# A one-core scan-and-gate kernel: the first loads, the first gate block and one square root are put in another order

## The chip, the cores and the metric

The kernel runs on one core of one Trainium2 chip. The metric is the device time of one execution in microseconds (us); lower is better. A line such as L826 is line 826 of the kernel file. TensorE is written PE (its weight loads PEld), VectorE DVE, ScalarE ACT, GpSimd POOL and SyncE SP. SP and ACT issue the loads that matter here; such an issue is written SPq or ACTq in the profile.

## The reference

The input is 2048 tokens of 448 numbers. After a layer norm, two branches read the same rows: a gated feed-forward block, and a diagonal complex recurrence over all tokens.

```
xn = layernorm(x)                                # x: 2048 x 448
g  = sigmoid(xn @ w_gate);  u = xn @ w_up        # w_gate, w_up: 448 x 1792
B  = silu((g * u) @ w_down)                      # w_down: 1792 x 448
h[t] = Lam_bar * h[t-1] + (xn @ B_bar.T)[t]      # complex, 448 states
A  = 2 * real(h @ C.T) + xn * Dskip
out = x + A * B
```

## The kernel before, in words

The tokens are cut into 4 chunks of 512, and each chunk into 4 tiles of 128 rows. PE works through chunk 0's gate products, then its up products, then the products of the recurrence, then the later chunks, nearly without a gap. The 1792 columns of `w_gate` are 14 blocks of 128, held as two halves: columns 0 to 895 lie on partitions 0 to 63 and columns 896 to 1791 on partitions 64 to 127. The 448 rows of the weights are seven row blocks `s` of 64 rows. A product `m` is a pair of streams, L808 with L809 (or L826 with L827), one on each half of the partitions, over the seven `s`.

The change lies in the head, the time until PE has its first full-width product (L808 on 512 columns, which starts at 10.71 us in the profile). What happens there:

- Loads of `x`, one for each 128-row tile 0 to 3, two issued by SP (0, 2) and two by ACT (1, 3).
- Gate block 0 (products `m` = 0 and 1, 256 columns of each half, 448 KB in all) comes in four pieces made by `load_w0`. Of half 0, part A holds `s` = 1, 3, 5 and part B `s` = 0, 2, 4, 6; of half 1 it is the other way round. The A pieces (96 and 128 KB) are what the "b" products of tile 0 read; the "a" products read the B pieces too. One A piece goes through ACT, the rest through SP.
- Gate blocks 1 (224 KB a half) and 2 (336 KB a half) follow on SP's queue, then more of `x`, then the up weights.
- Tiles 0, 2 and 3 get their mean and variance on DVE (`bn`, L451; `aggr`, L457). Tile 1 gets them on ACT: `act_mean` (L489) and `act_var` (L493), each a pass over 448 columns.
- The standard deviation of a tile is a small ACT instruction: `root` (L485), or `act_root` (L497) for tile 1. DVE then takes the reciprocal (`recip`, L482) and writes the normalised tile (`norm`, L531).
- PE transposes the normalised tile 0 (L569, L571). ACT copies slots 4 to 6 out of PSUM first, and slots 0 to 3 second (both L579, "copy b" and "copy a" in this text). With copy b, PE can do tile 0's "b" products (L826, L827 with `s` = 1, 3, 5), with copy a the "a" products.
- Between the two groups of products PE transposes tile 1 (L589, L590), behind them tiles 2 and 3, each copied out by ACT (L593); DVE shifts rows for tiles 1 to 3 (L600). Then come the products of tiles 1, 2 and 3.
- A small copy on ACT (L642, `pv`) feeds a chain on POOL (L653 to L659) whose result two ACT passes (`scale`, L669) need; behind these ACT loads its silu table (L665) and clears the first gate products from PSUM (L842).

While `pl.seq` is true (from `stats(0)` to `scale(3)`), the order of the instructions on DVE and ACT is the order of the Python calls; PE's order is always that, and so are SP's and ACT's loads. All the rest on DVE, ACT and POOL is put in order by a planner, `Plan.solve`, from costs and due times. For loads, the planner takes the landing time that `land=` names; it sets an order, not a time on the chip. A load issued by SP or ACT uses one of eight semaphores in turn, so the ninth waits until the first has landed.

Of the kernel before, what the change touches and what calls it, by code (L numbers as in the profile page):

```python
# [14 lines left out]
ACT = mybir.ActivationFunctionType  # L15
# [5 lines left out]
P = 128  # L21
H = 64
# [51 lines left out]
class Plan:  # L74
# [10 lines left out]
    def add(self, eng, cost, fn, r=(), w=(), dma=0, lat=None, chain=False, name="", rate=230e3):  # L85
        o = Op()
        o.idx, o.eng, o.cost, o.fn, o.dma, o.name = len(self.ops), eng, cost, fn, dma, name
        o.lat = LAT.get(eng, 0.0) if lat is None else lat
        o.pre, o.suc, o.rate = {}, [], rate
        o.slot, o.land = None, 0.0  # L90
        if dma and eng != "POOL":
            o.slot, self.n_dma = self.n_dma, self.n_dma + 1
        o.start = o.end = None
        for k in r:
            if k in self.w:
                self._edge(self.w[k], o, True)
        for k in w:
            for q in self.r.get(k, ()):
                self._edge(q, o, False)
            if k in self.w:  # L100
                self._edge(self.w[k], o, True)
        for k in w:
            self.w[k] = o
            self.r[k] = []
        for k in r:
            if k not in w:
                self.r.setdefault(k, []).append(o)
        if chain or eng == "PE" or (eng in ("DVE", "ACT") and self.seq):
# [138 lines left out]
def kernel(  # L247
# [18 lines left out]
    V, A, G, T, Q = nc.vector, nc.scalar, nc.gpsimd, nc.tensor, nc.sync  # L266
# [5 lines left out]
    def sbt(name, shape, dt=BF16):  # L272
        return sb.tile([P] + list(shape), dt, name=name)
# [10 lines left out]
    wgt = {"g": sbt("wG", [7, 896]), "u": sbt("wU", [7, 896])}  # L284
    wsrc = {"g": B_w_gate, "u": B_w_up}
# [5 lines left out]
    xnT = [flat(t[:], 7, L) for t in xnT_raw]  # L291
# [55 lines left out]
    gu = [pp.tile([P, 2, 512], FP32, name=f"gu{i}") for i in range(3)]  # L347
# [3 lines left out]
    add = pl.add  # L351
# [14 lines left out]
    def load_w(eng, k, half, b, r=(), rate=105e3, land=0.0):  # L366
        m0, m1 = BLK[k][b]
        ps = slice(half * H, half * H + H)
        c0 = half * 896
        load(eng, [("w", k, half, m) for m in range(m0, m1)], H * 7 * (m1 - m0) * P * 2,  # L370
             wgt[k][ps, :, m0 * P:m1 * P],
             wsrc[k][:, c0 + m0 * P:c0 + m1 * P].rearrange("(s p) f -> p s f", p=H), cost=0.65, r=r, rate=rate, land=land)

    def load_w0(eng, half, part, r=(), land=0.0):
        ps = slice(half * H, half * H + H)
        s0, c0 = (1 - half if part == "A" else half), half * 896
        n = 4 - s0
        load(eng, [("w", "g", half, m, part) for m in range(2)], H * n * 2 * P * 2, wgt["g"][ps, s0:7:2, 0:2 * P],
             wsrc["g"][:, c0:c0 + 2 * P].rearrange("(s p) f -> p s f", p=H)[:, s0:7:2, :], cost=0.5, r=r, rate=400e3, land=land)

    def wkeys(k, m, part=None):
        if k == "u" or m > 1:
            return [("w", k, 0, m), ("w", k, 1, m)]
        if part == "b":
            return [("w", k, 0, m, "A"), ("w", k, 1, m, "A")]
        return [("w", k, h, m, q) for h in range(2) for q in "AB"]

    def load_wd(h):
        fs = slice(h * 7, h * 7 + 7)
# [11 lines left out]
    def load_p(eng, k, r=()):  # L401
        load(eng, ("vrow", k), D * 2, vrow[k:k + 1, :], (A_log_dt, A_Lambda_im, A_Lambda_re)[k].unsqueeze(0), cost=0.75 if eng == "POOL" else 0.45, r=r)
    load_x(0, 1, "SP")
    load_x(1, 1, "ACT")
    load_x(2, 1, "SP", rate=180e3)
    load_x(3, 1, "ACT", rate=180e3)
    load_p("SP", 2)
    add("ACT", 0.05, lambda: A.preload_act_table_set("sqrt_and_others"), w=["sqrttab"], lat=1.3, chain=True)
    load_w0("SP", 0, "A", land=5.7)
    load_w0("ACT", 1, "A", land=5.9)  # L410
    load_w0("SP", 0, "B", land=6.9)
    load_w0("SP", 1, "B", r=[("x", 1)], land=6.9)
    load_p("POOL", 0)
    load_p("POOL", 1)
    add("POOL", 0.15, lambda: G.memset(ident[:], 0.0), w=["ident"], chain=True)
    add("POOL", 0.4, lambda: G.affine_select(out=ident[:], in_=ident[:], compare_op=ALU.not_equal, fill=1.0, base=0,
                                             pattern=[[-1, P]], channel_multiplier=1), r=["ident"], w=["ident"], chain=True)
    add("POOL", 0.1, lambda: G.memset(wgt["g"][0:1, 0, 256:258], 0.0), w=[("w", "g", 0, m) for m in (2, 3)], chain=True)
    load_w("SP", "g", 0, 1, rate=400e3, land=8.8)
    load_w("SP", "g", 1, 1, rate=400e3, land=9.8)  # L420
    load_w("SP", "g", 0, 2, rate=400e3, land=11.2)
    load_w("SP", "g", 1, 2, rate=400e3, land=12.6)
    load_x(4, 2, land=14.0)
    add("POOL", 0.1, lambda: G.memset(halfc[:], 0.5), w=["consts"])
    add("POOL", 0.1, lambda: G.memset(negc[:], -1.0), r=["consts"], w=["consts"])
    add("POOL", 0.1, lambda: G.memset(expc[:], math.e), w=["expc"])
# [5 lines left out]
        w=[("xnw", t) for t in (1, 2, 3)])  # L432
# [26 lines left out]
    def stats(t):  # L459
        bn(t)  # L460
        aggr(t)
# [22 lines left out]
    def root(t):  # L484
        add("ACT", 0.2, lambda: A.activation(sdb[:, t, :], mvf[:, t, 1:2], ACT.Sqrt, bias=epsc[:]),  # L485
            r=[("mv", t), "sqrttab", "epsc"], w=[("sd", t)], lat=0.16)

    def act_mean(t):
        add("ACT", 0.62, lambda: A.activation(junk[:], x_all[:, t, :], ACT.Identity, scale=-1.0 / D, accum_out=nmf[:, t, :]),  # L489
            r=[("x", t), "sqrttab"], w=[("nf", t), "junk"])  # L490
# [324 lines left out]
    def last_tile(c, k, steps, j, hs="ba"):  # L815
        x, w_ = xnT[c % 3], wgt[k]
        ts = slice(j * P, j * P + P)
        for h in hs:
            ss = {"a": (0, 2, 4, 6), "b": (1, 3, 5), "c": (0, 2, 4), 1: (6,)}[h]
            for m, a in steps:  # L820
                ms = slice(m * P, m * P + P)

                def f(ms=ms, a=a, ss=ss):
                    for s in ss:
                        go, end = (s == 1, s == 6) if hs[0] == "b" or hs == "a" else (s == 0, s == 5)
                        T.matmul(gu[a][:, 0, ts], lhsT=w_[0:H, s, ms], rhs=x[0:H, SL[s], ts], start=go, stop=end)  # L826
                        T.matmul(gu[a][:, 1, ts], lhsT=w_[H:P, (s + 1) % 7, ms], rhs=x[H:P, SL[s], ts], start=go, stop=end)  # L827
                add("PE", len(ss) * 0.0562, f, r=[("xnT", c % 3, j, "a" if h == "c" else h)] + wkeys(k, m, "b" if h == "b" else "a"), w=[("gu", a)],
                    name=f"{k}{c}.{m}")

    sg_n = [0]
# [227 lines left out]
    def yout(c, j, first=False):  # L1059
        t = c * TPC + j  # L1060
        g, o, q = gt_of[c, j], next_o(), t % NXD
        a = next_acc()
        key, ok, od = ("acc", a), ("o", o, 0), o_t[o][:]
        y = y_mm(c, j, acc[a], key, 0, D, False, first)
        add("DVE", dve1(D), lambda: V.tensor_tensor(out=od, in0=y, in1=xd[q][:], op=ALU.add), r=[key, ("xd", q)], w=[ok])
        add("DVE", dve2(D), lambda: V.tensor_tensor(out=od, in0=od, in1=g_t[g][:], op=ALU.mult), r=[ok, ("gt", g)], w=[ok])
        add("DVE", dve2(D), lambda: V.tensor_tensor(out=od, in0=od, in1=x_all[:, t, :], op=ALU.add), r=[ok, ("x", t)], w=[ok])
        rows = (0, H, P) if c == 2 and j == 3 else (0, P)
        for r0, r1 in zip(rows, rows[1:]):
            store(t, od, 0, D, r0, r1, [ok])  # L1070

# [31 lines left out]
    u2 = slots0[2]  # L1103
    gate([("gu", u2)], [("gu", u2, 0), ("gu", u2, 1)])
    stats(0)
    act_mean(1)
    bn(2)
    root(0)
    act_var(1)
    recip(0, 1)  # L1110
    aggr(2)
    norm(0)
    act_root(1)
    root(2)
    stats(3)
    recip(1, 1)
    norm(1)
# [1 line left out]
    def split(t, keys, banks, eng, between=None):  # L1119
        pe_transpose(t, [(4, 7, keys[0], banks[0], eng[0]), (0, 4, keys[1], banks[1], eng[1])], between)  # L1120
# [5 lines left out]
    def between_copies():  # L1126
        copies.append(columns(acc[1][:, 400:412], ("acc", 1)))
        last_tile(0, "g", steps01, 0, "b")
        root(3)
    split(0, ak, ab, ("ACT", "ACT"), between_copies)  # L1130
    copies[0]()
    add("NONE", 0.0, lambda: None, r=["pv0", ("xn", 1)], w=["pv"], lat=0.0)
    first_slots(1, uk[0], ub[0], "ACT")
# [94 lines left out]
    a = next_acc()  # L1228
# [37 lines left out]
```

## Time and profile before

| | |
|---|---|
| three runs | 182.92, 183.3, 183.31 us; median 183.3 |
| profiled execution: span, first to last instruction | 181.5 us |
| median of the runs above that span | 1.8 us |
| PE busy | 177.1 us, 98% of the span |
| DVE, ACT, POOL busy | 92%, 54%, 21% |
| granted TensorE clock | 1.00 throughout |
| PE idle in the last stage, 170 to 181.5 us | 3.07 us of 11.5 |

The profile gives no device time of the profiled execution besides its span, so sums are made against that span and carried over to the median of the runs by their difference.

How to read what follows: in the timeline an entry gives start, duration, engine, line, what it writes and reads, and in brackets how long the engine sat idle before it and what ended that. In the table of stretches each engine has its busy time in the stretch.

### The profile page before, as it was taken

The page shows a single profiled execution, that of the slowest core. Times are in us where ns is not written, and L with a number is a line of the kernel's source. Part 1 is how long each engine was busy: PE and PEld are TensorE (multiplying, and loading weights), DVE is VectorE, ACT ScalarE, POOL GpSimd, SP SyncE. Part 2 cuts the span into 40 slices and gives each one's busy share as a digit, 9 for nine tenths or more (in the row PEclk, how much of TensorE's full clock was granted, in tenths as well). Part 3 has the DMA queues.
Part 4 walks back from the last instruction along what each step waited for, and adds up shares of the span by engine and source line. Part 5 has one row for each costly group of instructions (what it writes and reads, how often), then busy time and mean ns, then how long its engine had stood idle before and what let it go on. Part 6 is the DMA issues. An engine that isn't in the chain of part 4 may idle for free.

```text
span 181.5 us, 3611 instructions
## 1 busy us (share of the span) xinstructions
PE 177.1 (98%) x1404; PEld 88.2 (49%) x1411; DVE 166.4 (92%) x294; ACT 98.2 (54%) x162; POOL 37.6 (21%) x94
## 2 busy tenths in 40 slices
PE   8999999999999999999999999999999999999993
PEld 2664445664544444445554444444555444455552
DVE  3778799999989999999999999999999999999772
ACT  5799998857699985364155543348110533411100
POOL 6472468100018797000004100000000000000000
PEclk9999999999999999999999999999999999999999
DMA  5999999999000290000004900002000000002121
GB/s 133 227 224 229 160 165 207 252 242 257 23 0 0 52 148 6 0 4 0 0 2 88 143 0 0 4 0 69 7 4 0 25 27 28 1 0 76 47 65 47
DMA packets 30853, 13.43 MB, mean 74 GB/s; under 512 B 19442, under 2 KB 30835, under 8 KB 30835
## 3 DMA queue, kind: packets, MB, share of 16 engines
q1 hardware_dynamic: 30210, 12.83, 34.9%
q10 hardware_dynamic: 560, 0.36, 0.7%
q8 instruction: 11, 0.18, 0.5%
q14 instruction: 8, 0.06, 0.1%
q0 software_dynamic: 64, 0.00, 0.0%
HBM read 6.77 MB, written 1.84 MB: 47 GB/s over the span
## 4 chain that ended last, share of the span: by engine, by line
PE 94%; DMA 2%; SPq 1%; DVE 1%; issue 0%; DVEq 0%
PE gu L808 43%; PE gu L1024 15%; PE acc L1043 11%; PE acc L1024 9%; PE gu L896 8%; DMA wG<-in_B_w_gate_dram 2%; PE acc L899 2%; PE gu L882 2%; SPq L357 1%; PE gu L826 1%; PE acc L808 1%; PE gu L809 1%; DVE o_t L1085 0%; PE gu L827 0%; DVE o_t L1079 0%
## 5 line engine op out<-in xcount | busy, mean ns | idle before, releaser
L808 PE MATMUL gu<-xnT,wU 64*128 64x512 bf16 x196 | 45.8, 376 | 0.0
L809 PE MATMUL gu<-xnT,wU 64*128 64x512 bf16 x196 | 45.8, 376 | 0.0
L808 PE MATMUL gu<-xnT,wG 64*128 64x512 bf16 (+1 forms) x189 | 41.3, 360 | 0.0
L809 PE MATMUL gu<-xnT,wG 64*128 64x512 bf16 (+1 forms) x189 | 41.3, 360 | 0.0
L842 ACT ACTIVATE sig<-gu 128x1024 f32<-128x1024 f32 x21 | 21.3, 1019 | 24.4 <-PE gu L809 19.8
L1024 PEld LDWEIGHTS <-hF 128*128 128x128 bf16 x224 | 21.9, 98 | 20.6
L808 PEld LDWEIGHTS <-wU 64*128 64x128 bf16 x196 | 18.4, 94 | 22.9
L808 PEld LDWEIGHTS <-wG 64*128 64x128 bf16 x196 | 18.4, 94 | 19.9
L1024 PE MATMUL gu<-wd,hF 128*128 128x448 bf16 x140 | 28.0, 352 | 0.0
L845 DVE SCALAR_TENSOR_TENSOR hF<-sig,gu 128x1024 bf16<-128x1024 f32 x21 | 25.4, 1210 | 0.7 <-ACT sig L842 0.4
L1043 PE MATMUL acc<-cT,hT 128*128 128x448 bf16 (+2 forms) x119 | 22.9, 337 | 0.0
L963 DVE TENSOR_TENSOR_SCAN wv<-c_r,st,z 128x512 bf16<-128x512 f32 x18 | 22.8, 1273 | 0.0
L1030 ACT ACTIVATE g_t<-gu 128x448 bf16<-128x448 f32 x10 | 5.4, 540 | 27.7 <-PE gu L1024 16.8
L809 PEld LDWEIGHTS <-wU 64*128 64x128 bf16 x196 | 18.4, 94 | 0.0
L809 PEld LDWEIGHTS <-wG 64*128 64x128 bf16 x196 | 18.4, 94 | 0.0
L1024 PE MATMUL acc<-wd,hF 128*128 128x448 bf16 x84 | 16.9, 352 | 0.0
L1043 PEld LDWEIGHTS <-hT 128*128 128x128 bf16 x126 | 11.7, 98 | 9.9 <-issue 0.4
L896 PE MATMUL gu<-xnT,bT 128*128 128x512 bf16 x65 | 15.3, 379 | 0.4
L910 ACT CAST bus<-gu 128x1024 bf16<-128x1024 f32 x12 | 12.0, 1011 | 5.9 <-PE gu L882 5.3
L541 POOL COPY xn<-xn 128x448 bf16<-128x448 bf16 x12 | 7.5, 627 | 27.2 <-ACT xn L535 27.0
L916 ACT CAST bus<-acc 64x256 bf16<-64x256 f32 (+1 forms) x24 | 8.7, 368 | 4.8 <-PE acc L899 4.5
L535 ACT ACTIVATE xn<-x_all,nmr,rsd 128x448 bf16<-128x448 bf16 x12 | 8.8, 758 | 3.7 <-DVE xd L546 2.2
(162 smaller groups left out, 263.1 us busy)
## 6 DMA issues: line engine op xcount, KB each, us to landing
wd<-in_B_w_down_dram SPq DMA_DIRECT2D x2, 784.0 KB, 6.6
out_dram<-o_t SPq DMA_DIRECT2D x14, 112.0 KB, 1.7
wU<-in_B_w_up_dram SPq DMA_DIRECT2D x4, 224.0 KB, 8.4
x_all<-in_A_x_dram SPq DMA_DIRECT2D x2, 448.0 KB, 5.0
wG<-in_B_w_gate_dram SPq DMA_DIRECT2D x2, 336.0 KB, 5.4
wU<-in_B_w_up_dram SPq DMA_DIRECT2D x2, 336.0 KB, 8.5
wG<-in_B_w_gate_dram SPq DMA_DIRECT2D x2, 224.0 KB, 4.1
x_all<-in_A_x_dram SPq DMA_DIRECT2D x2, 224.0 KB, 7.7
```

Source lines behind the costliest of these rows:

```text
L535: add("ACT", 0.65, lambda: A.activation(o[:, 0:448], x_all[:, t, :], ACT.Identity, bias=nmr[:, t, :], scale=rsd[:, t, :]), r=[("x", t), (" ...
L541: add("POOL", 0.25 if n == H else 0.6, lambda: G.tensor_copy(out=o[:, D:D + n], in_=o[:, 0:n]), r=[("xn", b)], w=[("xnw", b)])
L808: T.matmul(bank[0][:, ts], lhsT=w_[0:H, s, ms], rhs=x[0:H, SL[s], ts], start=(s == 0), stop=(s == 6))
L809: T.matmul(bank[1][:, ts], lhsT=w_[H:P, (s + 1) % 7, ms], rhs=x[H:P, SL[s], ts], start=(s == 0), stop=(s == 6))
L842: add("ACT", act(1024), lambda: A.activation(th, gu[a][:], ACT.Tanh, scale=0.5), r=[("gu", a)], w=[tk])
L845: add("DVE", dve1(1024), lambda: V.scalar_tensor_tensor(out=ho, in0=th, scalar=1.0, in1=gu[a][:], op0=ALU.add, op1=ALU.mult), r=[("gu", a) ...
L896: T.matmul(gu[slots[pt]][:, i, :], lhsT=bT[:, kt, i, pt * P:pt * P + P], rhs=x[:, kt, :], start=(first and kt == 0), stop=(not first and k ...
L910: add("ACT", act(1024), lambda: A.copy(out=bus[u][:], in_=gu[slots[pt]][:]), r=key(pt), w=[("bus", u)])
L916: add("ACT", 0.36, lambda ns=ns, d=d, q=q, l=l, i=i: A.copy(out=bus[u][d, l, ns], in_=acc[a3[i]][q, 0:256]), r=[("acc", a3[i])] + ([("bus" ...
L963: dve(1.194, lambda k=k: V.tensor_tensor_scan(out=wv[:, k, :], data0=rb, data1=z[:, k, :], initial=(st[pt][:, k, :] if c else 0.0), op0=AL ...
L1024: T.matmul(d, lhsT=hF[c % 2][:, m, h, js], rhs=wd[:, ft, :], start=(ft == 0), stop=(ft == FT - 1))
L1043: T.matmul(y, lhsT=hT[c % 2][:, hm, js], rhs=cT[:, cm, c0:c1], start=(i == 0 and not skip_on_pe), stop=(i == 6))
```

## The change

Six edits, all but the last in the head:

1. A new load goes first on ACT's queue: 16 partitions by 7 row blocks by 32 columns of `w_gate` into an unused tile `scr`. Its rows are every fourth row of the weights, 64 bytes of each.
2. The four `x` loads are issued in the order 0, 2 on SP and 1, 3 on ACT; on ACT they stand behind the new load, and tile 3's behind the table load.
3. Gate block 0 comes as two whole halves of 224 KB, half 0 on SP and half 1 on ACT, in place of the four pieces. Every product of it now waits for both halves. The `land` times of the planner are lower by 1.2 to 1.4 us for what follows.
4. POOL's two-element memset that held back gate block 1 is gone.
5. On ACT, tile 0's `root` goes ahead of `act_mean(1)`; tile 2's goes from ahead of copy b to between copy b and copy a; tile 3's from there to behind copy a.
6. At the end, the output of tile (2, 2) is stored as two halves of 64 rows, as that of (2, 3) is already.

```diff
-    def load_w0(eng, half, part, r=(), land=0.0):
...
-    def wkeys(k, m, part=None):
-        if k == "u" or m > 1:
-            return [("w", k, 0, m), ("w", k, 1, m)]
-        if part == "b":
-            return [("w", k, 0, m, "A"), ("w", k, 1, m, "A")]
-        return [("w", k, h, m, q) for h in range(2) for q in "AB"]
+    def wkeys(k, m):
+        return [("w", k, 0, m), ("w", k, 1, m)]
...
     load_x(0, 1, "SP")
-    load_x(1, 1, "ACT")
-    load_x(2, 1, "SP", rate=180e3)
-    load_x(3, 1, "ACT", rate=180e3)
+    scr = sbt("scr", [7, 32])
+    load("ACT", "scr", 16 * 7 * 64, scr[0:16, :, :],
+         B_w_gate.rearrange("(s e r) f -> r e s f", s=7, r=4)[0][:, :, 0:32], cost=0.5)
+    load_x(2, 1, "SP", land=3.7)
+    load_x(1, 1, "ACT", land=3.5)
     load_p("SP", 2)
     add("ACT", 0.05, lambda: A.preload_act_table_set("sqrt_and_others"), w=["sqrttab"], lat=1.3, chain=True)
-    load_w0("SP", 0, "A", land=5.7)
-    load_w0("ACT", 1, "A", land=5.9)
-    load_w0("SP", 0, "B", land=6.9)
-    load_w0("SP", 1, "B", r=[("x", 1)], land=6.9)
+    load_x(3, 1, "ACT", land=4.3)
+    load_w("SP", "g", 0, 0, rate=400e3, land=5.6)
+    load_w("ACT", "g", 1, 0, rate=400e3, land=5.6)
+    load_w("SP", "g", 0, 1, rate=400e3, land=7.6)
+    load_w("SP", "g", 1, 1, rate=400e3, land=8.6)
...
-    add("POOL", 0.1, lambda: G.memset(wgt["g"][0:1, 0, 256:258], 0.0), w=[("w", "g", 0, m) for m in (2, 3)], chain=True)
-    load_w("SP", "g", 0, 1, rate=400e3, land=8.8)
-    load_w("SP", "g", 1, 1, rate=400e3, land=9.8)
-    load_w("SP", "g", 0, 2, rate=400e3, land=11.2)
-    load_w("SP", "g", 1, 2, rate=400e3, land=12.6)
-    load_x(4, 2, land=14.0)
+    load_w("SP", "g", 0, 2, rate=400e3, land=10.0)
+    load_w("SP", "g", 1, 2, rate=400e3, land=11.4)
+    load_x(4, 2, land=12.6)
...
-        rows = (0, H, P) if c == 2 and j == 3 else (0, P)
+        rows = (0, H, P) if c == 2 and j > 1 else (0, P)
...
     stats(0)
+    root(0)
     act_mean(1)
     bn(2)
-    root(0)
     act_var(1)
     recip(0, 1)
     aggr(2)
     norm(0)
     act_root(1)
-    root(2)
     stats(3)
...
         last_tile(0, "g", steps01, 0, "b")
-        root(3)
+        root(2)
     split(0, ak, ab, ("ACT", "ACT"), between_copies)
+    root(3)
     copies[0]()
```

More of the change, by code (lines that the diff above doesn't have):

```diff
@@ L372, in load_w @@
              wsrc[k][:, c0 + m0 * P:c0 + m1 * P].rearrange("(s p) f -> p s f", p=H), cost=0.65, r=r, rate=rate, land=land)
-    def load_w0(eng, half, part, r=(), land=0.0):
[L375 to L379, printed above, removed]
-    def wkeys(k, m, part=None):
-        if k == "u" or m > 1:
-            return [("w", k, 0, m), ("w", k, 1, m)]
-        if part == "b":
-            return [("w", k, 0, m, "A"), ("w", k, 1, m, "A")]
-        return [("w", k, h, m, q) for h in range(2) for q in "AB"]
+    def wkeys(k, m):
+        return [("w", k, 0, m), ("w", k, 1, m)]
     def load_wd(h):
@@ L827, in f @@
                         T.matmul(gu[a][:, 1, ts], lhsT=w_[H:P, (s + 1) % 7, ms], rhs=x[H:P, SL[s], ts], start=go, stop=end)
-                add("PE", len(ss) * 0.0562, f, r=[("xnT", c % 3, j, "a" if h == "c" else h)] + wkeys(k, m, "b" if h == "b" else "a"), w=[("gu", a)],
+                add("PE", len(ss) * 0.0562, f, r=[("xnT", c % 3, j, "a" if h == "c" else h)] + wkeys(k, m), w=[("gu", a)],
                     name=f"{k}{c}.{m}")
```

## The prediction

> **What bounds the kernel now.** I read the page's busy table first, then the stretches of the head, then the chain of waits, then each engine's timeline of the head.
>
> ```profile
> PE 177.1 (98%) x1404; PEld 88.2 (49%) x1411; DVE 166.4 (92%) x294; ACT 98.2 (54%) x162; POOL 37.6 (21%) x94
> ```
> ```profile
> 6.00:7.00 1.00, 0.93 (x19) 0.67 (x17) 0.93 (x5) 0.82 (x5) 0.04 (x1) 1.00 0.86 220
> 7.00:8.00 1.00, 0.86 (x20) 0.65 (x20) 0.65 (x3) 0.57 (x1) 1.00 (x1) 1.00 1.16 272
> 8.00:9.00 1.00, 1.00 (x32) 0.90 (x31) 0.35 (x2) 0.77 (x2) 0.68 (x4) 1.00 0.98 215
> ```
>
> PE is the bound: from 8.35 us, where tile 1's products begin, to 170 us it is idle for 0.36 us (0.16, 0.10, 0.05 and 0.05 us of the stretches from 30 us on). So the change is worth what it shifts that start. PE's own idle time between 6 and 8 us is 0.21 us, but the head is also a chain of other engines' steps, and this chain is what the change reorders.
>
> ```profile
> 3.47 3.74 DMA wG<-in_B_w_gate_dram
> 7.25 0.23 PE gu L827
> ```
> ```profile
> 7.25 0.09 PEld L827 LDWEIGHTS <-wG 64*128 64x128 bf16 x1 [0.28 <-DMA wG<-in_B_w_gate_dram]
> ```
>
> The chain that ended last goes through the fourth piece of gate block 0: issued at 3.47 us, landed at about 7.21. PE had tile 0's "a" products ready at 6.87 and could go on at 7.25. Before that, the pace is ACT's:
>
> ```profile
> 3.28 0.58 ACT L489 ACTIVATE junk<-x_all 128x448 bf16<-128x448 bf16 x1 [0.34 <-DMA x_all<-in_A_x_dram]
> 4.06 0.30 ACT L485 ACTIVATE sdb<-mvf,epsc 128x1 bf16<-128x1 f32 x1
> 4.26 0.65 ACT L493 ACTIVATE junk<-x_all,nmf 128x448 bf16<-128x448 bf16 x1
> 5.03 0.30 ACT L497 ACTIVATE sdb<-sqf,epsc 128x1 bf16<-128x1 f32 x1
> 5.23 0.28 ACT L485 ACTIVATE sdb<-mvf,epsc 128x1 bf16<-128x1 f32 x1
> 5.57 0.48 ACT L579 COPY xnT<-acc 128x384 bf16<-128x384 bf16 x1
> 6.15 0.57 ACT L579 COPY xnT<-acc 128x512 bf16<-128x512 bf16 x1
> ```
>
> Tile 1's mean (3.28) runs while ACT waits for tile 0's variance; the root of tile 0 (4.06) comes the moment that DVE has it (L457, 3.77 to 3.95).
>
> **The change, part by part.** *Tile 0's root first.* It can't start earlier: its input is ready at 3.95 whatever stands ahead of it. But the mean of tile 1 now comes behind it, at 4.06 + 0.20 = 4.26 (0.20 is the step from one root to the next instruction, 4.06 to 4.26), in place of 3.28. Mean to end of its accumulator is 0.67 (3.28 to 3.95), so the variance pass starts at 4.95; pass to tile 1's root is 0.77 (4.26 to 5.03), so that root is at 5.72 and copy b, which stands behind it, at 5.92 in place of 5.57: **+0.35**. Tile 2's root no longer stands ahead of copy b; that is in the 5.92. Copy a follows copy b at 0.58 (5.57 to 6.15, a root between them then as now): 6.50. On PE the "b" products follow copy b by 0.54 (5.57 to 6.11): 6.46; tile 1's transposes 0.44 later (6.11 to 6.55): 6.90; the "a" products 0.32 later (6.55 to 6.87): 7.22. Copy a ends at 7.07, in time.
>
> *The DMA wait.* The "a" products no longer wait for a fourth piece, only the "b" products for the whole block. They ran on from 7.25, now from 7.22: the 0.38 us from 6.87 to 7.25 goes, and the 0.35 of ACT takes its place. **Net −0.03.**
>
> *The arrivals of `x`.* Tile 0 of `x` no longer shares the DMA engines with tile 1, which is issued some 0.45 us later behind the small load. Its 112 KB took 2.4 us from issue to landing beside tile 1's 112 KB; at 274 GB/s (stretch 2 to 3 us) the other 112 KB are 0.4 us of traffic. So it gains 0 to 0.4 us, and more only if the last engine is as fast as the first (the trace's landing updates for tile 0 run from 2.58 to 3.09). Against it stand the small load's 112 rows on the same engines: packets of 56 bytes took about 10 ns in the packet records, but first packets of `x` and of the gate weights took 300 to 450 ns on single engines; one such stall costs up to 0.4. I take −0.1, ends −0.5 and +0.4. Tile 1 may land as late as 4.23 before it holds its mean; issued second on ACT, it lands between 3.7 (its own 2.5 us from an issue at 1.2) and 4.07 (when the second load of ACT's queue landed before). Covered by 0.2.
>
> *Block 0 in two halves.* The "b" products need 448 KB where they needed 224. Nearest rows:
>
> ```profile
> wG<-in_B_w_gate_dram SPq DMA_DIRECT2D x2, 224.0 KB, 4.1
> wG<-in_B_w_gate_dram SPq DMA_DIRECT2D x2, 96.0 KB, 3.9
> wG<-in_B_w_gate_dram ACTq DMA_DIRECT2D x1, 128.0 KB, 4.2
> ```
>
> A load of the same 224 KB takes 4.1. Half 0 keeps SP's place at 2.02: lands at 6.1. Half 1 stands fourth on ACT: 0.73 plus an issue of 0.41 to 0.69 (the rows of a `x` load and of a weight piece there) plus two of 0.45, and gaps: 2.15 to 2.45, so it lands at 6.25 to 6.55. PE asks at about 6.45. The middle, 6.40, is just in time: **0**, ends 0 and +0.75 (a landing at 7.20, as before).
>
> Does the small load warm anything? Eight packets over 300 ns stand at 3.4 to 4.4 us, when the first gate pieces flow, but nine more at 5.5 to 8.4, after the four pieces had been through every row block. I credit it with nothing.
>
> *What is covered.* Gate block 1's issue comes forward from 4.20 to about 3.1, since SP has two pieces fewer ahead and the ninth load waits for tile 0's landing (3.1); its product starts at 10.7 and it had landed by 9.2: nothing to gain there. The gone memset ended at 3.15: nothing. Tile 2's root is now at 6.40; its norm (7.2) is asked for at 7.8. Tile 3's root, behind copy a at 6.96, gives its norm by 7.95, asked for at 7.98: covered by 0.03, and it moves with ACT. The `pv` copy goes from 6.61 to about 7.15, so POOL's chain (6.96 to 8.94), the two passes at 9.19, the table load at 10.56 and the first clearing of a bank (11.85 to 12.87) all go some 0.5 later; PE wants that bank at 13.7: 0.85 of cover, 0.35 left. If it were gone, each 0.1 would be on PE. The extra half store is issued at 168.9; the last two halves took 0.58 and 1.31 us on SP, and SP's next store comes at 173.2: nothing.
>
> **Sum** against the profiled execution: −0.38 + 0.35 − 0.1 + 0 = −0.13, of which I keep half, since block 0's landing would take back what tile 0 gains beyond 0.05 us. 181.5 becomes 181.4; the runs' median lies 1.8 above the span, so 183.3 becomes 183.25 us. A difference under 0.2%, 0.37 us, is about what a measurement of this kernel can tell from no change.
>
> **The rivals.** *Block 0 comes late (slower).* SP's gate block 1 is now issued at 3.1, so once half 0 is through, block 1's packets run beside half 1's, while before the fourth piece had its 96 KB on the queue ahead of block 1. And a load lands with its slowest engine: the first SP piece, 96 KB issued at 2.02, had engines done from 4.49 to 6.05. The price is the landing less 6.45; it decides from 6.45, passes 0.37 at 6.82, and at 7.20 gives +0.75: 184.0. For it: no 224 KB load of the head landed under 4.0 us. Against it: both halves are issued by 2.45, the fourth piece at 3.47.
>
> The Trainium skill, "DMA: Bandwidth & Descriptors", section "Issuing engines are not separate DMA queues", says that loads from different engines run on the same 16 DMA engines and interleave, and that another issuer only saves issue time. The trace agrees: ACT's 128 KB piece and SP's 96 KB piece, issued 0.3 us apart, took 4.2 and 3.9. By it, half 1 on ACT's queue has no bandwidth of its own beside block 1, which speaks for this rival.
>
> *Everything arrives early (faster).* Tile 0 lands near its first engine's 2.6, tile 2 early too, and block 0 before 6.0: copy b returns to 5.57 or 5.45, and the whole 0.38 to 0.5 is kept: 182.85. For it: `x` meets less traffic. Against it: it needs weights faster than any row of this trace.
>
> *The small load doesn't do what it says, and harms.* Its stalls, up to 0.45 each on an engine, fall among the first packets of tiles 0 and 2: tile 0 at 3.4 to 3.5, all of ACT's chain with it, +0.3 to +0.4: 183.65.
>
> **How the numbers follow.** Nothing to speak of, 0.45 (own range 182.95 to 183.65); block 0 late, 0.30, two thirds of it beyond 0.37; early, 0.17; harm by the small load or by an order of the planner's that turns out worse on DVE or ACT, 0.08. The faster case counts as faster, and 0.02 of scatter with it: 0.19. Slower: 0.2 and 0.08 and some for scatter and for covers of 0.03 and 0.35 us, that are thin: 0.35. The rest, 0.46, is within 0.2%. The range reaches to the early case, 182.85, and to the late block, 184.05.
>
> **What would show it.** The first 512-column product (L808), at 10.71 before: at 10.65 if I am right, 11.1 or later if block 0 is late, 10.3 if all is early. Tile 1's mean (L489) should start at 4.2, copy b (L579) at 5.8 to 5.9, and the "a" products show no DMA wait. A wait of PE's L826 on the gate weights at the "b" products is the first rival; a first `bn` (L451) later than 3.11 is the third. PE idle of more than 0.6 us after 30 us would mean that I missed an effect of the new order behind the head.

## The result, and the profile after

| | before | changed |
|---|---|---|
| median of the runs | 183.27 us (182.92 to 183.31, 4 runs) | 185.81 us (184.13, 185.72, 185.89, 187.3) |
| ratio | 1 | 1.0112, 95% interval 1.009 to 1.0133 |
| profiled execution: device time, span | span 181.5 us | 184.13 us, span 182.4 us |

The change makes the kernel slower by about 1%. The run of 187.3 us lies more than 1.5% above the fastest and is left out of the ratio. The others fall into two groups, which the mean granted TensorE clock tells apart: it is 1.000 in the run of 184.13 us and 0.991 in those of 185.72 and 185.89 us. The profiled execution is the first of these, so its profile shows only one of the two losses: 0.86 us of 2.5. The line numbers below are those of the changed kernel, 11 lower than before (L815 for L826, L797 for L808, L568 for L579).

The busy table hardly moves, as a PE that waits a little in the head must look over 182 us:

```profile
PE 177.2 (97%) x1404; PEld 88.4 (48%) x1411; DVE 166.4 (91%) x294; ACT 98.0 (54%) x162; POOL 35.2 (19%) x93
```

The stretches of the head (start:end, length, then busy time of PE, PEld, DVE, ACT, POOL, the granted clock, the DMA share, GB/s) show the place. From 6 to 7 us PE is busy for 0.17 us, where it was 0.93 before:

```profile
6.00:7.00 1.00, 0.17 (x5) 0.08 (x3) 0.92 (x3) 1.00 (x5) 0.00 (x0) 1.00 1.18 251
7.00:8.00 1.00, 0.90 (x16) 0.63 (x16) 0.56 (x2) 0.07 (x2) 0.77 (x1) 1.00 1.18 237
8.00:9.00 1.00, 1.00 (x26) 0.82 (x24) 0.20 (x1) 0.59 (x1) 0.74 (x4) 1.00 1.13 232
```

The waits of PE's weight loads in the first 30 us (us in total, times, longest) name the cause, and the chain of waits gives its start:

```profile
PEld L815 <- DMA wG<-in_B_w_gate_dram: 0.9, 1, 0.9
...
PEld L816 <- DMA wG<-in_B_w_gate_dram: 0.2, 1, 0.2
```
```profile
1.17 0.45 ACTq L357
1.65 0.45 ACT L399
2.14 5.13 DMA wG<-in_B_w_gate_dram
7.31 0.23 PE gu L816
```

L815 is the first "b" product on half 0, L816 on half 1. So "b" now waits for both halves. Half 0, issued by SP at 2.01, is there at 6.94; half 1, issued by ACT at 2.14, at 7.27. PE's timeline shows the wait, and the first 512-column product 0.83 us later than 10.71:

```profile
6.99 0.23 PE L815 MATMUL gu<-xnT,wG 64*128 64x128 bf16 x1 [0.83 <-DMA wG<-in_B_w_gate_dram]
7.31 0.23 PE L816 MATMUL gu<-xnT,wG 64*128 64x128 bf16 x1
...
11.54 0.38 PE L797 MATMUL gu<-xnT,wG 64*128 64x512 bf16 x1
```

ACT is not to blame. Its order is the new one, and both copies out of PSUM are ready before the weights:

```profile
3.80 0.30 ACT L474 ACTIVATE sdb<-mvf,epsc 128x1 bf16<-128x1 f32 x1 [0.87 <-DVE mvf L446]
4.00 0.56 ACT L478 ACTIVATE junk<-x_all 128x448 bf16<-128x448 bf16 x1
...
4.69 0.67 ACT L482 ACTIVATE junk<-x_all,nmf 128x448 bf16<-128x448 bf16 x1
...
5.48 0.30 ACT L486 ACTIVATE sdb<-sqf,epsc 128x1 bf16<-128x1 f32 x1
5.68 0.46 ACT L568 COPY xnT<-acc 128x384 bf16<-128x384 bf16 x1
...
6.24 0.57 ACT L568 COPY xnT<-acc 128x512 bf16<-128x512 bf16 x1
```

The DMA issues (KB each, median us from issue to landing) and SP's queue (start, time spent issuing) close the picture: half 1 took 5.1 us on ACT's queue, half 0 took 4.9 on SP's (the 5.1 shown there is the median of half 0 and the two halves of block 1), and SP issued its gate loads, block 1 and 2 among them, back to back from 2.01 to 5.66 us, where in the kernel before block 1 began at 4.20.

```profile
wG<-in_B_w_gate_dram SPq DMA_DIRECT2D x3, 224.0 KB, 5.1
...
wG<-in_B_w_gate_dram ACTq DMA_DIRECT2D x1, 224.0 KB, 5.1
```
```profile
2.01 3.65 SPq L357 DMA_DIRECT2D wG<-in_B_w_gate_dram  x5
```

**A count of bytes.** Four `x` tiles and block 0 are 448 + 448 KB, 918 thousand bytes. Summing the GB/s of the one-us stretches from 1 us on gives what had gone over the engines when the last of block 0 landed. Before: 42 + 274 + 197 + 222 + 173 + 220 and 0.21 of 272 up to 7.21 us, 1185 thousand. Changed: 33 + 199 + 236 + 146 + 318 + 251 and 0.27 of 237 up to 7.27, 1247 thousand. So some 270 and 330 thousand bytes of other loads went ahead of block 0's last rows; next in SP's queue stands block 1. Both kernels get the whole of block 0 at about the same time; the kernel before needs only its first half (the A pieces) for the "b" products.

### The profile page after: what moved, and what is told of

Same layout as the page of the kernel before. It is cut to its first block, busy times and chain, and to the rows that moved or that the text cites. A ratio compares the mean times of both kernels' runs of the same rounds, so it can differ in the third digit from the quotient of the medians.

```text
span 182.4 us, 3610 instructions
## 1 busy us (share of the span) xinstructions
PE 177.2 (97%) x1404; PEld 88.4 (48%) x1411; DVE 166.4 (91%) x294; ACT 98.0 (54%) x162; POOL 35.2 (19%) x93
## 4 chain that ended last, share of the span: by engine, by line
PE 94%; DMA 3%; DVE 1%; ACTq 0%; issue 0%; ACT 0%; DVEq 0%
PE gu L797 43%; PE gu L1013 15%; PE acc L1032 11%; PE acc L1013 9%; PE gu L885 8%; DMA wG<-in_B_w_gate_dram 3%; PE acc L888 2%; PE gu L871 2%; PE gu L815 2%; PE acc L797 1%; PE gu L798 1%; ACTq L357 0%; DVE o_t L1074 0%; PE gu L816 0%; DVE o_t L1068 0%
## 5 line engine op out<-in xcount | busy, mean ns | idle before, releaser
L797 PE MATMUL gu<-xnT,wU 64*128 64x512 bf16 x196 | 45.8, 376 | 0.0
L797 PE MATMUL gu<-xnT,wG 64*128 64x512 bf16 (+1 forms) x189 | 41.3, 360 | 0.0
L797 PEld LDWEIGHTS <-wU 64*128 64x128 bf16 x196 | 18.4, 94 | 22.9
L797 PEld LDWEIGHTS <-wG 64*128 64x128 bf16 x196 | 18.4, 94 | 19.9
```

What stands on the lines that cost most here:

```text
L797: T.matmul(bank[0][:, ts], lhsT=w_[0:H, s, ms], rhs=x[0:H, SL[s], ts], start=(s == 0), stop=(s == 6))
```

## The experiments

Two theories of the loss stood, and one rival. **Late block**: the "b" products wait for 448 KB that share the engines with block 1, and this costs 0.8 us and no more. **Clock**: PE's pause of about 1 us in the head makes the chip grant half the clock for a while afterwards, in most executions, and this costs the other 1.7. **Small load or order**: the new small load or ACT's new order does harm of its own. In the expectations below, theory 1 is the late block ("with the clock" adds the second), theory 2 is the small load, and theory 3 says that the lower clock has nothing to do with PE's pause. The time of the kernel before beside each set of runs was 183.0 to 183.2 us.

### Does waiting for all of block 0 alone cost 0.8 us?

**e8: the kernel before, with two small matmuls that read pieces 3 and 4 ahead of the "b" products.**

```diff
+        def probe():
+            for i, hs, s in ((0, slice(0, H), 2), (1, slice(H, P), 3)):
+                T.matmul(gu[u2][:, i, 0:128], lhsT=wgt["g"][hs, s, 0:P], rhs=wgt["g"][hs, s, 0:P], start=True, stop=True)
+        add("PE", 0.0, probe, w=uk)
```

> The kernel before, with two 128-column matmuls ahead of tile 0's b products that read the third and fourth piece of block 0 (their result is thrown away), so that PE goes on only when all 448 KB have landed, as the changed kernel's first products do. (In the earlier run of this idea only the planner's keys were changed; the chip's waits come from what an instruction reads, so nothing moved.) Theory 1: first product at 7.25 in place of 6.1, later end +0.77, and PE pauses for 1.2 us, so the clock is cut in some runs: the fast ones at 184.0, others at 185.5 to 186. Theory 3, the clock has nothing to do with PE's pause: all at 184.0.

Measured: 183.98 us (183.76 to 184.26, 4 runs), ratio 1.0045 (1.0031 to 1.0059): +0.8 us. The waits of PE's weight loads in this kernel show one for the probe, and PE is idle for 0.89 us until 7.35:

```profile
PEld L1131 <- DMA wG<-in_B_w_gate_dram: 1.0, 1, 1.0
```

So the wait for the whole block, without any other part of the change, reproduces the first loss. None of the four runs showed the second, though theory 1 expected it in some: their mean clock is 1.000. The pause was 0.89 us, and not the 1.2 that the expectation had.

**e4: the same wait, attempted by the keys alone.**

```diff
     def wkeys(k, m, part=None):
...
-        if part == "b":
-            return [("w", k, 0, m, "A"), ("w", k, 1, m, "A")]
```

> The kernel before, where only the wait is changed: tile 0's first products wait for all four pieces of block 0 and not for two. Theory 1: they start at 7.25 in place of 6.11, of which 0.38 was waited for later anyway: +0.77, 184.05 in runs at full clock; PE pauses for 1.2 us, so the clock falls in some or all runs and these give 185.7 or more. Theory 3: +0.77 and clock 1.00 throughout. Theory 2 says nothing of this one beyond +0.77.

Measured: 183.26 us (183.04 to 183.59, 10 runs), ratio 1.0005 (0.9996 to 1.0015). The experiment missed: the waits on the chip come from what an instruction reads, and the keys only feed the planner, so nothing changed. e8 is its replacement.

**e2: the changed kernel without the small load.**

```diff
-    scr = sbt("scr", [7, 32])
-    load("ACT", "scr", 16 * 7 * 64, scr[0:16, :, :],
-         B_w_gate.rearrange("(s e r) f -> r e s f", s=7, r=4)[0][:, :, 0:32], cost=0.5)
```

> The changed kernel without the small load; tile 1 of x is then first on ACT's queue again. Theory 1: block 0 is still 448 KB that must land whole, and lands at 6.8 to 7.3; PE still pauses by 0.6 us or more, 183.9 to 185.9. Theory 2, the small load is the harm: block 0 lands by 6.4, 183.2 to 183.4 with the clock at 1.00.

Measured: 185.02 us (184.14, 184.46, 185.59, 185.87), ratio 1.0104 (1.006 to 1.0147). Half 0 landed at 7.51 and half 1 at 7.24, in place of 6.94 and 7.27, and PE was idle for 1.19 us; both groups of runs are still there. So the small load is not the harm. Nor do the traces show that it warms anything: with it, slow packets of 551 to 674 ns still stood among the gate weights at 4.0 to 4.3 us, and in e14 and e15 below, with the small load, the halves landed at 7.34 to 7.61. Without it, tile 0 of `x` landed at 3.21 in place of 2.84, since tile 1 then runs beside it again.

**e5: the changed kernel, with block 1 held by a small POOL copy until half 1 has landed.**

```diff
+    add("POOL", 0.1, lambda: G.tensor_copy(out=wgt["g"][0:1, 0, 256:258], in_=wgt["g"][H:H + 1, 0, 0:2]),
+        r=[("w", "g", 1, 0)], w=[("w", "g", 0, m) for m in (2, 3)])
```

> The changed kernel, but gate block 1 is held back: a two-element copy on POOL reads half 1 of block 0 and writes into block 1's place, so SP issues block 1 (and all that is queued behind it) only when half 1 has landed. Theory 1a, block 1's packets beside half 1's are what makes block 0 late: both halves land by 6.2 to 6.5, PE's pause is under 0.3 us, first product at 6.3 to 6.5. Theory 1b, block 0 is late by itself (late start on ACT's queue, slow first packets): half 1 still lands at 7.0 or later. The later loads are 3 us behind in either case and may hold PE at the second gate block (10.7), so the landing and the first product decide here, not the time.

Measured: 185.88 us (185.34 to 186.15, 4 runs), ratio 1.0144 (1.0127 to 1.0161), and yet it answers the question. The halves landed at 6.47 and 6.63, 0.5 and 0.6 us earlier than in the first profile of the changed kernel, with block 1 beside them. The pause was 0.71 us, and not under 0.3, since PE was ready at 5.80. The bytes up to 6.63 are 26 + 244 + 224 + 201 + 218 and 0.63 of 15: 922 thousand, `x` and block 0 and hardly anything else. The time is lost afterwards: the DMA engines stood nearly still until past 8 us (15, 0 and 46 GB/s in the stretches from 6, 7 and 8 us), and PE waited for blocks 1 and 2 (for 0.29 and 1.15 us). The stretch from 6 to 7 us, and PE's waits in the first 30 us (L817 is the first "b" product, L800 the 512-column one):

```profile
6.00:7.00 1.00, 0.48 (x12) 0.42 (x12) 0.93 (x4) 1.00 (x5) 0.25 (x1) 1.00 0.06 15
```
```profile
PE gu L800 <- DMA wG<-in_B_w_gate_dram: 1.4, 2, 1.1
...
PE gu L817 <- DMA wG<-in_B_w_gate_dram: 0.7, 1, 0.7
```

So of the 0.83 us, 0.5 to 0.6 is block 1, and what follows it in SP's queue, on the same engines. Both figures compare single executions; beside e14 and e15 below, whose halves landed later, the gain is 0.9 to 1.0 us. The rest is the landing of 448 KB itself, 0.2 us behind the moment (6.4) for which I had it.

**e3: the changed kernel with the four pieces in place of the two halves.**

```diff
-    load_w("SP", "g", 0, 0, rate=400e3, land=5.6)
-    load_w("ACT", "g", 1, 0, rate=400e3, land=5.6)
+    load_w0("SP", 0, "A", land=5.6)
+    load_w0("ACT", 1, "A", land=5.6)
+    load_w0("SP", 0, "B", land=5.6)
+    load_w0("SP", 1, "B", land=5.6)
```

> The changed kernel with block 0 in the four pieces of the kernel before, issued in its order (SP, ACT, SP, SP) at the places of the two halves; the small load, the order of x and the order of the roots stay as changed. Theory 1: the first products need only the two first pieces, start at 6.2 to 6.3 behind copy b, PE does not pause for more than 0.2 us: 183.0 to 183.5, clock 1.00. Theory 2: the small load is still there, the pieces land late too, 183.9 or more.

Measured: 183.97 us (183.71 to 184.34, 4 runs), ratio 1.0042 (1.0025 to 1.0059). This undoes two thirds of the loss, but not cleanly: with the small load in front, ACT's A piece became the ninth load and waited for a semaphore until 3.09 us in place of 1.69, landing at 7.09. PE was idle twice, 0.36 and 0.65 us, and never for 0.8 us at a stretch. By its time alone this is what theory 2 forecast; but the small load did its harm here through its semaphore, for which none of ACT's loads waits in the changed kernel.

### Is the other 1.7 us the clock?

**e14 and e15: the changed kernel again, nothing edited**, to catch one of the longer executions in a profile.

> The changed kernel once more, for more runs beside the kernel before and one more trace. Theory 1 with the clock: two groups of runs, near 184.2 and near 185.8, some with 187; a trace of the second group shows PE's head at half speed for one window of 3.4 us that a trace of the first does not show. Theory 3: no such stretch in either.

> The changed kernel, one more trace; as for the run before this one.

Measured: e14 185.8 us (186.04, 185.85, 185.75, 184.09, 185.4, 186.15), ratio 1.0139 (1.011 to 1.0168); e15 a single run of 185.98. Both profiled executions were of the longer kind, with a mean clock of 0.988 and 0.991. The same stretches for e14, and for e15 from 8 us; the third number from the right is the granted clock. The last fence has the stretch from 10 to 11 us of the first profile of the changed kernel:

```profile
9.00:10.00 1.00, 1.00 (x18) 0.80 (x18) 0.58 (x2) 0.70 (x3) 0.90 (x6) 0.63 1.09 212
10.00:11.00 1.00, 1.00 (x24) 1.00 (x22) 0.89 (x4) 1.00 (x3) 1.00 (x2) 0.50 1.14 233
11.00:12.00 1.00, 1.00 (x24) 1.00 (x20) 0.94 (x3) 0.98 (x3) 0.71 (x3) 0.50 1.15 181
12.00:13.00 1.00, 1.00 (x30) 1.00 (x26) 0.96 (x3) 1.00 (x1) 0.00 (x0) 0.66 1.19 200
```
```profile
8.00:9.00 1.00, 1.00 (x21) 0.81 (x18) 0.00 (x0) 0.47 (x1) 0.76 (x3) 0.68 1.08 224
9.00:10.00 1.00, 1.00 (x16) 0.80 (x11) 0.57 (x2) 0.11 (x1) 0.90 (x5) 0.50 1.12 228
```
```profile
10.00:11.00 1.00, 1.00 (x44) 1.00 (x40) 0.90 (x4) 1.00 (x3) 1.00 (x2) 1.00 1.14 227
```

PE reads as fully busy in all of these, but e14 does 24 matmuls from 10 to 11 us where the first profile has 44. The trace's clock records give the edges: in e14 full speed is granted from 5.85 us, half from 9.26 to 12.68, then full again; in e15 full from 4.95, half from 8.36 to 11.77. Each piece is 3.41 us long. A stretch of 3.41 us at half speed loses at most 1.7 us. In both, the 3.41 us before the cut hold PE's pause for block 0: 1.18 us in e14 and 1.52 in e15, where the block landed at 7.60 and 7.61, against 0.83 in the first profile, which has no cut and a landing at 7.27. The first 512-column product comes at 13.45 us in e14, 1.91 later than in the first profile: 0.33 of that is the later landing and 1.6 the clock.

**e1: the changed kernel with five constant matmuls that fill PE's pause.**

```diff
+        def fill():
+            for _ in range(5):
+                T.matmul(gu[u2][:, 0, 0:512], lhsT=ones[:, 0:P], rhs=ones[:, 0:512], start=True, stop=True)
+        add("PE", 0.0, fill, w=[uk[0]])
```

> The changed kernel, with five full-width matmuls on constants put on PE between the small pv products and tile 0's first products (their result is thrown away). They fill 1.1 us of the 0.83 us that PE sat idle there in the changed kernel's profile. Theory 1, late block and clock: block 0 still lands at 7.0 to 7.3, so the first product starts no earlier and the fast end stays at 184.1 to 184.3; but PE does not pause, so the granted clock is 1.00 in every run and the runs at 185.7 to 185.9 are gone. Theory 2, the small load disturbs the DMA engines and that is all: nothing changes, 184.1 to 187. Theory 3, the lower clock of the other runs has nothing to do with the pause: 0.98 to 0.99 stays in most runs, and the median near 185.8.

Measured: 184.37 us (184.27, 184.35, 184.4, 184.64), ratio 1.0071 (1.0056 to 1.0086). The weights are as late as ever (7.10 and 7.39 us), but the group at 185.7 is gone, and the mean clock is 1.000 in all four runs. PE's timeline of this kernel:

```profile
5.82 1.26 PE L1119 MATMUL gu<-const-bfloat16-1.0 128*128 128x512 bf16 x5
7.14 0.23 PE L815 MATMUL gu<-xnT,wG 64*128 64x128 bf16 x1
7.43 0.23 PE L816 MATMUL gu<-xnT,wG 64*128 64x128 bf16 x1
```

Useless work in a wait that remains makes the changed kernel 1.4 us faster by the medians. Four runs are few, but of the other kernel's ten, without the one of 187.3 us, eight were at 185.4 or above.

**e10: the kernel before with a longer pause, made by a matmul that reads gate block 1 ahead of the "b" products; e11: the same with four filling matmuls in front.**

```diff
+        def fill():                                # e11 only
+            for _ in range(4):
+                T.matmul(gu[u2][:, 0, 0:512], lhsT=ones[:, 0:P], rhs=ones[:, 0:512], start=True, stop=True)
+        add("PE", 0.0, fill, w=[uk[0]])
+        def probe():
+            T.matmul(gu[u2][:, 0, 0:128], lhsT=wgt["g"][0:H, 0, 256:384], rhs=wgt["g"][0:H, 0, 256:384], start=True, stop=True)
+        add("PE", 0.0, probe, w=[uk[0]])
```

> The kernel before with one 128-column matmul ahead of tile 0's first products that reads gate block 1 (it landed at 8.2; the result is thrown away): PE pauses from 6.0 to 8.2, longer than in the changed kernel, and nothing else is changed. The pause itself puts the end off by 8.2 - 6.1 less the 0.38 of later waiting: +1.7 to +1.8, 184.9. Theory 1 with the clock: on top of that the clock is cut for a window in most runs and those are at 186.5 or more, and the trace shows a granted clock under 1 in the head. Theory 3: all runs at 184.9, clock 1.00.

> The same pause with four full-width matmuls on constants in it. Theory 1 with the clock: all runs at 184.9 to 185.2, none at 186.5. Theory 3: the same as without them.

Measured: e10 187.71 us (186.47 to 187.87, 5 runs), ratio 1.0231 (1.0208 to 1.0255); e11 185.28 us (185.14 to 185.71, 4 runs), ratio 1.0117 (1.0103 to 1.0132). The two resume at about the same time (8.08 and 8.42 us); four filling matmuls ahead of the pause are worth 2.4 us. The stretch from 10 to 11 us in e10, then in e11:

```profile
10.00:11.00 1.00, 1.00 (x16) 0.80 (x13) 0.57 (x2) 0.17 (x1) 1.00 (x2) 1.00 1.11 231
```
```profile
10.00:11.00 1.00, 1.00 (x32) 0.90 (x31) 0.69 (x3) 0.77 (x2) 0.97 (x2) 1.00 1.10 221
```

Half as many matmuls pass in e10. Its clock column says 1.00 all the same: the trace has its first clock record at 13.54 us, and the column shows nothing of the time before it. In e11 full speed is granted from 3.82 us. This late grant is the profiled execution of e10 (187.36 us) alone: its other four runs have a mean clock of 0.979 to 0.991, so in them half speed is on record. Counted back from 13.54 in pieces of 3.41 us, PE was busy for shares of 0.87, 0.60 and 1.00 of the three pieces before the grant: e10's pause lies in the first two of them, and the grant came behind the third. In e11 the piece before the grant has 0.89.

**e9: e8 with five filling matmuls in front.** Its edit is e8's probe behind e1's `fill`.

> The same, with five full-width matmuls on constants ahead of the two readers, which fill 1.1 us of the pause. Theory 1 with the clock: all runs at 184.0 to 184.2, none at 185.5 or more. Theory 3: the same as without the filler.

Measured: 184.53 us (184.09 to 184.65, 4 runs), ratio 1.0069 (1.0055 to 1.0083): slower than e8. In its profile the five matmuls ran from 6.32 to 7.67 us, the first for 0.38 us, ahead of the grant of full speed at 6.67, the others for 0.22 each; the weights had landed at 6.82. So the filling itself held the products for 0.85 us. e8 had lost nothing to the clock, so there was nothing to win either.

### ACT's new order alone

**e6: the kernel before with only the order of the roots changed.**

```diff
     stats(0)
+    root(0)
     act_mean(1)
...
-    root(0)
...
-    root(2)
...
-        root(3)
+        root(2)
...
+    root(3)
```

> The kernel before with the new order of the roots alone (tile 0's ahead of act_mean(1), tile 2's between the copies, tile 3's behind). By my sum, copy b comes 0.35 later, at 5.9, the first b products at 6.46, the a products at 7.22, which is when the fourth piece has landed anyway: within 0.1 of before, 183.1 to 183.3. If the order of the roots has a price of its own that the late weights hid in the changed kernel, it is slower by 0.3 or more.

Measured: 183.42 us (183.32 to 183.48, 11 runs), ratio 1.001 (1.0002 to 1.0019): +0.2 us. In its timeline tile 0's root is at 4.22 us, mean 4.42, copy b 6.10. From root to copy b it takes 1.88 us, where the kernel before takes 1.51 (4.06 to 5.57): 0.37 of order, for a forecast of 0.35. The root itself was 0.16 later here with `x`. PE:

```profile
6.61 0.21 PE L826 MATMUL gu<-xnT,wG 64*128 64x128 bf16 x1 [0.57 <-ACT xnT L579]
```

That PE comes 0.5 later to the "b" products costs only 0.2, since the fourth piece's wait at the "a" products is gone: they go on at 7.38, in place of 7.25. The expectation had the time within 0.1 of before.

### Versions that were to beat both

**e7: the fourth piece on ACT, without its wait for tile 1.**

```diff
-    load_w0("SP", 1, "B", r=[("x", 1)], land=6.9)
+    load_w0("ACT", 1, "B", land=6.9)
```

> The kernel before, where the fourth piece of block 0 (96 KB) is issued by ACT behind its first piece, without the wait for tile 1 of x, so at about 2.4 us in place of 3.47. By theory 1 what counts is only when the last piece that a product reads has landed: the piece lands at 6.2 to 6.6 in place of 7.2, the a products need not wait, and 0.2 to 0.38 us go: 182.8 to 183.0 against 183.18 of before. If a piece on ACT's queue only takes the bandwidth of the two pieces that the b products read, they land later by as much, and it stays at 183.2 or goes above.

Measured: 183.7 us (183.44 to 184.74, 11 runs), ratio 1.0039 (1.0025 to 1.0053). The piece is the ninth load and waits for the semaphore of tile 1's load, which landed at 3.44; so it is issued at 3.46, as in the kernel before, and not at 2.4. ACT's own work stands behind the issue, which ends at 4.09, and tile 0's root comes at 4.72 in place of 4.06. The piece landed at 8.01, and PE waited for it as well (0.46 us). The first line below holds both of ACT's gate issues, with the wait between them:

```profile
1.69 2.40 ACTq L357 DMA_DIRECT2D wG<-in_B_w_gate_dram  x2
4.14 0.58 ACT L489 ACTIVATE junk<-x_all 128x448 bf16<-128x448 bf16 x1 [1.20 <-DMA x_all<-in_A_x_dram]
...
4.72 0.28 ACT L485 ACTIVATE sdb<-mvf,epsc 128x1 bf16<-128x1 f32 x1
```

**e12: the same as an eighth load, the small `Lambda_re` load moved to POOL, and the split last store.**

```diff
-    load_p("SP", 2)
...
-    load_w0("SP", 1, "B", r=[("x", 1)], land=6.9)
+    load_w0("ACT", 1, "B", land=5.9)
...
+    load_p("POOL", 2)
...
-        rows = (0, H, P) if c == 2 and j == 3 else (0, P)
+        rows = (0, H, P) if c == 2 and j > 1 else (0, P)
```

> A try for a version that beats both: the kernel before, the four pieces of block 0 kept, but the fourth issued by ACT behind its first piece, and the small load of Lambda_re moved to POOL, so that the fourth piece is the eighth load and not the ninth: it no longer waits for a semaphore (in the run before this, ACT waited for one with the issue, and all its arithmetic behind it). The last store but five is in two halves, to keep the number of loads and stores. By theory 1 the fourth piece lands at 6.2 to 6.6, the a products start at 6.88 in place of 7.25: 182.8 to 183.0. If the four pieces share the engines to the same end, the third lands later and it is within 0.1 of before.

Measured: 183.27 us (182.95 to 184.04, 12 runs), ratio 1.0007 (0.9996 to 1.0018). All pieces landed by 6.63 and no product waited for weights. But the small load, now third on POOL, landed at 5.97, and PE's small products that read it hold the "b" products behind them:

```profile
6.11 0.21 PE L635 MATMUL acc<-ident,hF 3*128 3x3 bf16 x3 [0.48 <-DMA hF<-in_A_Lambda_re_dram]
```

**e13: half 1 whole on ACT at 1.7 us, half 0 in two pieces on SP, and the split last store.**

```diff
-    load_w0("ACT", 1, "A", land=5.9)
-    load_w0("SP", 0, "B", land=6.9)
-    load_w0("SP", 1, "B", r=[("x", 1)], land=6.9)
+    load("ACT", [("w", "g", 1, m, q) for m in range(2) for q in "AB"], H * 7 * 2 * P * 2, wgt["g"][H:P, :, 0:2 * P],
+         wsrc["g"][:, 896:896 + 2 * P].rearrange("(s p) f -> p s f", p=H), cost=0.5, rate=400e3, land=5.9)
+    load_w0("SP", 0, "B", land=6.3)
```

> The kernel before with block 0 in three pieces: half 1 whole on ACT (224 KB, issued at 1.7), half 0 in its two pieces on SP; eight loads in all, so none waits for a semaphore; block 1 is issued at about 3.5 in place of 4.2. If a whole half needs only to be issued early, it lands by 6.4, the b products wait 0.3 more than before, the a products none: 183.0 to 183.2. If block 1's packets beside it are what delays a half on ACT's queue, it lands at 6.8 or later: 183.4 or more, and slow runs through the clock are possible.

Measured: 183.12 us (183.02 to 183.82, 11 runs) against 183.0 for the kernel before, ratio 1.001 (1.0001 to 1.0019). Its profile has what the change was after: the last piece landed at 6.88, PE was idle for 0.14 us before the "b" products, and the span is 181.3 us against 181.5 in the profile of before. The runs don't confirm the 0.2 us. No version tried beats the kernel before.

## Why the prediction was wrong

**The bound, and what a shift is worth: right.** The first 512-column product moved by 0.83 us and the profiled execution's time by 0.86 (184.13 against 183.27). After 30 us PE's idle time is as it was.

**Tile 0's root first, +0.35: right.** The root came at 3.80, the mean 0.20 behind it, copy b at 5.68, that is 1.88 behind the root as worked out (5.92 less 4.06 is 1.86); e6 alone gives 1.88 too. Copy b stood at 5.68 and not 5.92 because `x` came earlier.

**The arrival of `x`, −0.1: sign right, size too small.** Tile 0 landed at 2.84 in place of 3.09, 0.25 earlier, inside the bounds. It bought nothing, because PE then waited for weights. The third rival, harm by the small load, is refuted by e2.

**Block 0 in two halves, taken at 0: the first of two steps that failed.** I priced each half by the median of two 224 KB loads, 4.1 us, and got 6.1 and 6.25 to 6.55; they took 4.9 and 5.1 us and landed at 6.94 and 7.27. The row was of loads issued behind block 0, and I had no term for what runs beside: I had noted that block 1 would be issued at 3.1 (it was, at 3.02, though the semaphore that it waited for was the small load's, landed at 3.00, and not tile 0's), called that "nothing to gain there", and kept its 448 KB out of the landing of half 1 in the sum; only the first rival had them. The stretches of the profile before already held an estimate: with nothing else in the queue, 42 + 274 + 197 + 222 + 173 from 1 to 6 us make 908 thousand of the 918, so 6.1 at best, and later by what block 1 takes of it. e5 puts the share of block 1 at 0.5 to 0.6 us beside the first profile.

The sentence of the Trainium skill that I set beside the first rival ("DMA: Bandwidth & Descriptors", "Issuing engines are not separate DMA queues": loads from several engines run on the same 16 engines and interleave) agrees with e5, in which half 1 on ACT's queue gained 0.6 us from holding SP's block 1. Of the two times that I set beside it, the 3.9 is the median of SP's two 96 KB pieces; the one issued at 2.02 took 4.0.

**The DMA wait, −0.38: right, and empty.** The "a" products no longer wait; the wait stands at the "b" products instead, and is longer. This is the first rival to the letter, PE's wait at L815 and L816. It had a chance of 0.30 and the price of +0.75 for a landing at 7.20; in the profiled execution the landing was 7.27 and the time +0.86.

**The clock: a term that the prediction does not have, the second step that failed, and the larger part of the loss.** The range ended at 184.05. Had the first rival been taken as the likeliest, 184.0 would have been the forecast, and the median is still 1.8 above it. I read the granted clock of 1.00 in the three stretches shown and asked only whether it was full, not what keeps it full. What the runs show: in e14 and e15 the half speed follows the pause by one piece of 3.41 us; filling the pause (e1) takes the loss away, the weights being as late as ever, and so does filling the front of a longer one (e11). In e14 the first 512-column product is 2.74 us later than in the kernel before (13.45 against 10.71): 0.83 as in the first profile, 0.33 for the later landing and 1.6 for the clock. The profile of before could not have given this price, for in it PE is never idle for more than 0.14 us between 6 and 8 us; it could have given a warning, the 427 ns between the first 512-column matmuls of the warm-up, twice the 216 of later ones. The "1.00 throughout" of my table does not cover them: the first clock record of that profile stands at 5.35 us.

**The covers: held.** From 7.31 us to 30 us PE shows no gap above 0.03 us; neither tile 3's norm (0.03 of cover) nor POOL's chain (0.35 left) came late. The extra half store was not measured alone.

**Still open:** how long a pause has to be. By PE's busy share in the 3.41 us that hold the pause, the profiles have cuts at 0.543 (e15) and 0.648 (e14), and none at 0.650 (e2), 0.653 (e11), 0.68 (e7), 0.70 (e3), 0.73 (the first profile of the changed kernel) and 0.74 (e8). All of them fit an edge just under 0.65, but two single profiles 0.002 apart can't fix it. The edges of these pieces stand at another time in each execution (full speed first came at 3.82 to 6.67 us in the profiles other than e10's), so one pause may fall into one piece or two. Why the halves landed 0.3 to 0.4 us earlier in the first profile than in e14 and e15 is open too.

## What to carry to other kernels

Cost the landing of a load by the bytes that will be in flight with it, from the earliest issue that the change allows, and not by the latency of a row of its size: moving a later load forward is a change to the earlier one. Here a first product that could start on part of a block was worth more than a shorter list of loads. And a new wait of PE of a microsecond or more near the start is to be priced twice, once for itself and once for the clock that may follow; where such a wait can't be removed, cheap matmuls in it can pay for themselves (e1), provided that they end before the wait does (e9).

## What the runs showed of the hardware

- In e14 and e15 a pause of PE of 1.18 and 1.52 us, soon after full speed was granted, was followed by one piece of 3.41 us at half speed, which cost some 1.6 us; in e2 a pause of 1.19 us was not. The Trainium skill ("TensorE: Matmul & The Clock Gate", "Part 1: The HAM clock gate") has a window of about 3.4 us for the gate, with which the 3.41 us agree, but a return to the lower clock only after a whole window of idle; here less than half a window of idle was enough (1.20 and 1.56 us of 3.41).
- In the profiled execution of e10, with a pause of 1.81 us and no full clock granted before it, full speed came only at 13.54 us. The clock column reads 1.00 before the first record, so the matmuls per microsecond have to be read beside it.
- A load that waits for its semaphore holds the engine that issues it, and with it that engine's arithmetic: in e7 ACT issued the waiting piece from 3.46 to 4.09 us, and its pass over tile 1, which had landed at 3.44, began at 4.14.
- The small load of 7 KB, 64 bytes a packet, did not keep slow packets (551 to 674 ns) from the gate weights that followed it.
